# Attention, soft mixture of experts and MLP on one core: four buffers for whole chunks of P, two for the light ones, four for x, and no quarter of expert weights loaded ahead

## The chip, the core and the metric

The kernel runs on one core of a Trainium2 chip. A core has five engines that each take their own instructions in order: PE (TensorE, matmuls; the profile lists its weight loads apart as PEld), ACT (ScalarE), DVE (VectorE), POOL (GpSimd) and SP (SyncE, which here only issues DMA transfers). Semaphores tie them together. The metric is the time of one execution on the device in microseconds (us), as the median of several runs. Before the change it is 596.64 us, the median of three runs from 596.44 to 599.81 us.

## The reference

Attention over 4 batches of 12 heads with 448 positions and 64 channels, with scores squeezed by a tanh; then a soft mixture of 8 experts with 4 slots each; then an MLP with a leaky activation. All in fp32.

```python
scores = cap * np.tanh(scale * (q @ k.T) / cap)
attn = np.exp(scores - scores.max(-1)); attn /= attn.sum(-1) + 1e-09
x = (attn @ v)                                    # to 1792 x 768
logits = x @ phi                                  # phi: 768 x 32 slots
d = softmax(logits, over tokens); c = softmax(logits, over slots)
slot_input = d.T @ x                              # 4 rows for each of 8 experts
slot_out[e] = np.maximum(slot_input[e] @ w1[e], 0.0) @ w2[e]
x = c @ slot_out
h = x @ w_in
out = (np.maximum(h, 0.0) + alpha * np.minimum(h, 0.0)) @ w_out
```

## The kernel before, in words

**Attention** takes the heads two at a time, 24 pairs in all. The 448 keys of a pair are cut into four chunks: three whole ones (0, 1, 2) of 128 keys, with both heads side by side in 896 columns, and a light one (3) that holds the last 64 keys of both heads in 448 columns. A step g does, for pair i and the next chunk in `CHUNKS = (0, 3, 1, 2)`: `qk` (three matmul passes into the PSUM tile `s`, of which there are two, then on ACT a tanh, L395, and an exp, L396, into a tile `p` of P), then what `later` put down for this step, then loads, and then, two steps behind (`LAG = 2`), `pv` of an older chunk: P times V into the one PSUM bank `o`. Step 1 of a pair also transposes the next pair's k and q (`tr`).

`pv` of chunk 1 makes POOL add up P for the row sums: `acc = p0 + p1` (L412, one add for each head) and then the light chunk's rows (L415); `pv` of chunk 2 adds the third whole chunk (L419). ACT then copies `o` to SBUF as `xu` (L421), and only then may PE write `o` for the next pair. The tiles of P come from two pools that are used in turn: `pt`, three buffers for whole chunks, and `ptt`, one buffer for light ones. A tanh may write a buffer when PE and POOL have read what was in it.

`xu` has five buffers. It is kept until `norm` (DVE, L502) multiplies it by the inverse row sums, which come for three pairs together: `norm` of pairs 0, 1, 2 falls on steps 20, 24 and 28.

In the background DVE and ACT convert `w_in` from float64, which passes through `cvbuf` (`conv_w_in`, L192 to L203), and SP loads q, k and v two pairs ahead.

**Weights.** The experts' weights (50 MB) go through eleven slots of 12 KB per partition in a pool `arena`. `LOADS` lists the pairs at whose last step a slot's load is issued, if a slot is free: ten are, and the eleventh (the one that holds `cvbuf`) comes free at pair 22. So the pairs that load are 2, 4, ... 20 and 22. Beyond the slots there is a quarter, `early` (one tile of 3 KB per partition), into which `load_early` loads the first quarter of the next piece (w2 of expert 2) at pair 21. All loads are on SP's queue. When attention ends, its memory becomes seven more slots (`xslots`), each filled as soon as what lay there is read for the last time (L119); from then on a slot that an expert has finished with is refilled at once.

**Tail.** `experts` runs the eight experts, `gather` turns the result, and `mlp` does the rest on PE, DVE and ACT. `mlp` uses a scratch tile `more`, for which it takes the memory of `early`.

Of the kernel before, what the change touches and what calls it, by code (L numbers as in the profile page):

```python
# [8 lines left out]
F32 = mybir.dt.float32  # L9
# [15 lines left out]
def tile_attention_soft_moe_mlp(ctx, tc, q, k, v, cap, phi, w1, w2, w_in, w_out, alpha, out):  # L25
# [5 lines left out]
    NPAIR = B * NP  # L31
    NT, DM = out.shape
# [9 lines left out]
    SLOT = 3072  # L42
    NA = 11
    NX = 7
    QE = 1
    JK = 3
    KEYS = 128 * JK
    TAIL = S - KEYS
# [3 lines left out]
    LAG = 2  # L52

    CHUNKS = (0, 3, 1, 2)
    LOADS = (2, 4, 6, 8, 10, 12, 14, 16, 18, 20, 21, 22)

    EH = 5
    TBS = (4, 2, 2, 2, 2, 2)
# [4 lines left out]
    arena = ctx.enter_context(tc.tile_pool(name="arena", bufs=1))  # L63
# [10 lines left out]
    slotT = const.tile([128, KD, NSLOT], F32, name="slotT")  # L74
    w_in32 = dram_p.tile([DFF // 512, DM, 512], F32, name="w_in32")
    xslots = []
    early = [arena.tile([128, SLOT // 4], F32, tag=f"early{c}", name="w") for c in range(QE)]

    def slot(i, shape, dtype=F32, name="w"):
        return arena.tile(shape, dtype, tag=f"slot{i}", name=name)  # L80
# [2 lines left out]
    loads, rest = [], []  # L83
# [11 lines left out]
    where = {}  # L95
# [18 lines left out]
    def load_part(kind, e, i, c, t, after=None):  # L114
        if kind == "w2":
            src = w2_rows(e, i)[:, c // 2, c % 2]
        else:
            src = w1_rows(e, i)[:, c]
        ins = nc.sync.dma_start(out=t, in_=src)  # L119
        if after is not None:  # L120
            tc.add_manual_dep(ins.ins, after.ins.name, NOSYNC, reason="prefetch pace")
        return t

    def load_early(after):

        key = loads[NA]
        where[key] = [load_part(*key, c, t, after) for c, t in enumerate(early)]

    def load_next(after=None):
        slot_no = may_load()  # L130
# [110 lines left out]
    def attention():  # L241
        with ExitStack() as pools:
            def pool(name, bufs=1, **kw):
                return pools.enter_context(tc.tile_pool(name=name, bufs=bufs, **kw))
# [4 lines left out]
            v_0 = pool("vn0")  # L249
            acc_0 = pool("acc0")  # L250
            stk_1 = pool("stk1")
            pt_p = pool("pt", 3)
            ptt_p = pool("ptt")
            v_1 = pool("vn1")
            acc_1 = pool("acc1")
            ac0_p = pool("aconst0")
            xn_p = pool("xn", 7)
            xu_p = pool("xu", 5)
            xnat_p = pool("xnat", 2)
            sm_p = pool("sm")  # L260
            ac_p = pool("aconst")
# [22 lines left out]
            nat, stk, sc_t, pt, acc, ov, xu, xn = {}, {}, {}, {}, {}, {}, {}, {}  # L284
# [399 lines left out]
            def cv_at(n):  # L684
                return cv_steps[n]
# [39 lines left out]
            last = None  # L725
            for g in range(NPAIR * J + LAG):
                now[0] = g
                i, c = divmod(g, J)
                if g == 14:
                    nc.sync.dma_start(out=alpha_sb, in_=alpha.rearrange("(k p) -> p k", p=128))  # L730
                if g == 17:
                    nc.vector.tensor_scalar(out=nalpha_sb, in0=alpha_sb, scalar1=-1.0, scalar2=None, op0=ALU.mult)
                if i < NPAIR:
                    qk(i, CHUNKS[c])
                    if c == 1 and i + 1 < NPAIR:
                        trans_k(i + 1)
                        trans_q(i + 1)
                run_bg()
                if i < NPAIR:
                    if c == 0:  # L740
                        last = load(i + 2, "kq") or last
                    if c == 2:
                        if i == NPAIR - LAG - 1:
                            load_early(last)
                    for n in range(ncv):
                        if cv_at(n) == g - 2:
                            store_w_in(n)
                        if cv_at(n) == g:
                            conv_w_in(n)
                    if c == 3 and i in LOADS and may_load() is not None:  # L750
                        load_next(last)
                if g >= LAG:
                    n, e = divmod(g - LAG, J)
                    pv(n, CHUNKS[e])
                    if e == J - 1:
                        load(n + 2, "v")
# [22 lines left out]
    def tail():  # L779
# [3 lines left out]
        def unit(n, dtype, name):  # L783
            return r2[0].tile([128, DM], dtype, tag=f"u{n}", name=name)
# [50 lines left out]
        def experts(which, small, ps_w, yacc, cstk=None):  # L835
            for e in which:
                if e == E - 1:
                    to_single(0)
                    split_wo(0)
                hT = small[:, 0:256].rearrange("p (u j s) -> p u j s", u=2, j=4)  # L840
                nc.gpsimd.memset(hT, 0.0)
                h1 = ps_w.tile([128, 512], F32, tag="w", name="h1")[:, :256]
                for kk in range(KD):
                    wv = where["w1", e, kk // 3]
                    for j in range(4):
                        nc.tensor.matmul(
                            h1[32 * j:32 * j + 32, :],
                            slotT[:, kk, :],
                            wv[kk % 3][:, 256 * j:256 * j + 256],
                            start=(kk == 0),  # L850
                            stop=(kk == KD - 1),
                            tile_position=(0, 32 * j),
                        )
                done_with("w1", e, 0)
                done_with("w1", e, 1)
                rl = small[:, 256:512]
                nc.scalar.activation(
                    out=rl.rearrange("q (u p) -> q p u", u=2), in_=h1.rearrange("q (p u) -> q p u", u=2), func=AF.Relu
                )
                tp = ps_w.tile([128, 512], F32, tag="w", name="tp")[:, :256]  # L860
                for u in range(2):
                    nc.tensor.transpose(tp[:, 128 * u:128 * u + 128], rl[:, 128 * u:128 * u + 128], ident)
                nc.vector.tensor_copy(
                    out=hT[:, :, :, SPE * e:SPE * e + SPE],
                    in_=tp.rearrange("p (u j s) -> p u j s", u=2, j=4)[:, :, :, SPE * e:SPE * e + SPE],
                )
                for kk in range(KE):
                    wv = where["w2", e, kk // 4]
                    for g in range(G3):
                        pe[0] = nc.tensor.matmul(  # L870
                            yacc[32 * g:32 * g + 32, :256],
                            hT[:, kk % 2, kk // 2, :],
                            wv[kk % 4][:, 256 * g:256 * g + 256],
                            start=(e == 0 and kk == 0),
                            stop=(e == E - 1 and kk == KE - 1),
                            tile_position=(0, 32 * g),
                        )
                done_with("w2", e, 0)
                done_with("w2", e, 1)
                if EH <= e < EH + B // 2:  # L880
                    for b in (2 * (e - EH), 2 * (e - EH) + 1):
                        build_c(b, ps_w, cstk)
# [433 lines left out]
        with (  # L1316
            tc.tile_pool(name="ps_w", bufs=2, space=PSUM, reuse_waits="tile") as ps_w,
            tc.tile_pool(name="ps_c", bufs=6, space=PSUM, reuse_waits="tile") as ps_c,
        ):
            yacc = ps_c.tile([128, 512], F32, tag="c", name="y")  # L1320
            with (
                tc.tile_pool(name="ex2", bufs=1, reuse_waits="tile", side="right") as ex2_p,
                tc.tile_pool(name="xtra", bufs=1, reuse_waits="tile") as xt_p,
            ):
                small = ex2_p.tile([128, 512], F32, name="small")
                xslots.append(xt_p)
                free.extend(range(NA, NA + NX))
                load_free()
                experts(range(EH), small, ps_w, yacc)
            with (  # L1330
                tc.tile_pool(name="r2", bufs=1, reuse_waits="tile") as r2_p,
                tc.tile_pool(name="ex", bufs=1, reuse_waits="tile") as ex_p,
                tc.tile_pool(name="gg", bufs=1, reuse_waits="tile") as g_p,
            ):
                r2.append(r2_p)
                so = ex_p.tile([128, KD, 2, NSLOT], F32, name="so")
                cstk = ex_p.tile([128, NT], F32R, name="cstk")
                a_stk = ex_p.tile([128, DFF], F32R, name="a_stk")
                gr = g_p.tile([128, 4096], F32R, name="gr")
                gs = g_p.tile([128, 2688], F32, name="gs")  # L1340
                ob = g_p.tile([128, 2, DM], F32, name="ob")
                experts(range(EH, E), unit(6, F32, "small"), ps_w, yacc, cstk)
                gather(ps_w, yacc, so)
                more = arena.tile([128, SLOT // 4], F32, tag="early0", name="more")
                mlp(ps_w, ps_c, so, cstk, a_stk, gr, gs, ob, more)

    attention()
    tail()


# [28 lines left out]
```

## Time and profile before

| | |
|---|---|
| median of three runs | 596.64 us |
| the profiled execution: its own time | 595.48 us |
| its span, first to last instruction | 593.6 us |
| PE busy | 554.3 us, 93% of the span |
| DVE / ACT / POOL busy | 433.9 / 377.4 / 169.4 us |
| attention, about 12 to 273 us | PE, ACT, DVE and POOL all work |
| experts, to 336 us | the 16 DMA engines are full |
| MLP, 339 us to the end | PE is full |

Busy time is a share over stages with different limits, so what a change is worth is read from its own stage. "Idle before" and the waits say what an engine waited for last; matmuls are pipelined and their ends are modelled. "PEclk" is the TensorE clock that was granted, as a share of 2.4 GHz.

### The profile page before, as it was taken

The numbers are of one execution on the slowest core, as the hardware profiler recorded it, in microseconds if no ns is written. First come the engines' busy times: TensorE is split into PE (matmuls) and PEld (weight loads), VectorE is DVE, ScalarE is ACT, GpSimd is POOL, SyncE is SP. The second block draws the span as 40 slices with busy tenths as digits, with TensorE's granted clock in tenths as the row PEclk, the third lists the DMA queues.
The fourth block names the chain that finished last, engine by engine and source line by source line (L and its number), as shares of the span: only waits on it lengthen the run. The fifth ranks groups of instructions, "written<-read, shape, count | busy, mean of one in ns | idle before, by whom it ended". The sixth has DMA issues, their size and how long they took to land.

```text
span 593.6 us, 10809 instructions
## 1 busy us (share of the span) xinstructions
PE 554.3 (93%) x4008; PEld 383.4 (65%) x4008; DVE 433.9 (73%) x834; ACT 377.4 (64%) x617; POOL 169.4 (29%) x158
## 2 busy tenths in 40 slices
PE   5979998999999999988888989999999999999996
PEld 4434444455545445445445568878888999999996
DVE  3688976788577958562011499999999979797974
ACT  3988888888888978831011157764777855565651
POOL 0786877766765656510000000000000000000000
PEclk9998999999999999999999999999999999999999
DMA  6577887888787784599999999500030101010101
GB/s 174 115 249 214 268 254 236 209 252 250 231 204 222 241 237 109 193 376 386 421 420 418 396 399 412 204 0 1 20 88 1 55 0 55 2 53 1 54 1 54
DMA packets 83461, 110.93 MB, mean 187 GB/s; under 512 B 55376, under 2 KB 63312, under 8 KB 81872
## 3 DMA queue, kind: packets, MB, share of 16 engines
q1 hardware_dynamic: 81168, 109.28, 55.8%
q10 hardware_dynamic: 2240, 0.95, 0.6%
q8 instruction: 32, 0.52, 0.4%
q14 instruction: 21, 0.17, 0.1%
HBM read 98.41 MB, written 11.80 MB: 186 GB/s over the span
## 4 chain that ended last, share of the span: by engine, by line
PE 66%; DMA 10%; ACT 10%; POOL 6%; DVE 3%; issue 2%; SPq 1%; ACTq 0%
DMA w<-in_moe_w_dram 9%; PE o L293 8%; PE s L293 7%; PE P L1204 6%; PE P L1206 6%; PE P L1205 6%; PE oc L979 6%; PE oc L985 6%; PE oc L986 6%; ACT p L396 3%; POOL acc L412 3%; POOL acc L415 3%; ACT p L395 2%; PE aps L907 2%; PE nx L293 2%
## 5 line engine op out<-in xcount | busy, mean ns | idle before, releaser
L293 PE MATMUL o<-p,v 128*64 128x448 f32 (+1 forms) x384 | 94.0, 568 | 11.1 <-ACT xu L421 11.0
L395 ACT ACTIVATE p<-s 128x896 f32<-128x896 f32 x96 | 79.1, 824 | 29.0 <-PE s L293 17.7
L396 ACT ACTIVATE p<-p,cap 128x896 f32<-128x896 f32 x96 | 91.1, 950 | 2.4
L412 POOL TENSOR_TENSOR acc<-p 128x448 f32<-128x448 f32 x48 | 58.0, 1230 | 68.3 <-ACT p L396 68.3
L985 PE MATMUL oc<-wsp,gr 128*128 128x512 f32 (+1 forms) x192 | 64.9, 339 | 0.0
L986 PE MATMUL oc<-wsp,gr 128*128 128x512 f32 (+1 forms) x192 | 64.2, 337 | 0.0
L979 PE MATMUL oc<-wsp,gr 128*128 128x512 f32 (+1 forms) x192 | 62.0, 340 | 0.0
L293 PEld LDWEIGHTS s<-qh,kh 64*128 64x128 f32 (+1 forms) x168 | 18.2, 187 | 67.3 <-issue 24.7
L1195 ACT ACTIVATE gr<-gs 128x384 fp32r<-128x384 f32 (+1 forms) x64 | 36.6, 575 | 32.8 <-DVE gs L1179 26.8
L415 POOL TENSOR_TENSOR acc<-acc,p 64x448 f32<-64x448 f32 x46 | 54.5, 1184 | 1.7
L419 POOL TENSOR_TENSOR acc<-acc,p 128x448 f32<-128x448 f32 x46 | 54.0, 1195 | 1.8
L1196 DVE TENSOR_TENSOR gr<-gs,gr 128x384 fp32r<-128x384 f32 x64 | 39.1, 619 | 17.4 <-ACT gr L1195 17.4
L293 PE MATMUL s<-qh,kh 64*128 64x448 f32 (+1 forms) x168 | 46.0, 476 | 0.0
L1204 PE MATMUL P<-wsp,gr 128*128 128x384 f32 x128 | 42.9, 335 | 0.0
L1205 PE MATMUL P<-wsp,gr 128*128 128x384 f32 x128 | 42.8, 334 | 0.0
L1206 PE MATMUL P<-wsp,gr 128*128 128x384 f32 x128 | 42.8, 334 | 0.0
L293 PEld LDWEIGHTS o<-p,v 128*64 128x64 f32 (+1 forms) x384 | 19.0, 134 | 36.3 <-ACT xu L421 17.8
L979 PEld LDWEIGHTS oc<-wsp,gr 128*128 128x128 f32 x192 | 36.2, 190 | 5.4 <-ACT wsp L814 0.8
L985 PEld LDWEIGHTS oc<-wsp,gr 128*128 128x128 f32 x192 | 36.4, 189 | 5.1 <-DVE wx L203 0.4
L986 PEld LDWEIGHTS oc<-wsp,gr 128*128 128x128 f32 x192 | 36.3, 189 | 4.4 <-issue 0.4
L293 PE MATMUL s<-ql,kh 64*128 64x448 f32 (+1 forms) x168 | 35.5, 366 | 1.0 <-DVE ql L375 1.0
L293 PE MATMUL s<-qh,kl 64*128 64x448 f32 (+1 forms) x168 | 35.6, 366 | 0.0
(234 smaller groups left out, 1228.3 us busy)
## 6 DMA issues: line engine op xcount, KB each, us to landing
w<-in_moe_w_dram SPq DMA_DIRECT2D x26, 768.0 KB, 12.5
w<-in_moe_w_dram SPq DMA_DIRECT2D x12, 1536.0 KB, 11.8
cvbuf<-in_moe_w_in_dram SPq DMA_DIRECT2D x24, 512.0 KB, 5.3
w<-in_moe_w_out_dram SPq DMA_DIRECT2D x16, 768.0 KB, 10.4
w_in<-cvbuf SPq DMA_DIRECT2D x24, 256.0 KB, 2.7
w<-in_moe_w_dram SPq DMA_DIRECT2D x12, 512.0 KB, 6.2
q<-in_q_dram SPq DMA_DIRECT2D x44, 112.0 KB, 4.1
k<-in_k_dram SPq DMA_DIRECT2D x48, 96.0 KB, 5.5
```

Source lines behind the costliest of these rows:

```text
L293: ins = nc.tensor.matmul(*a, **kw)
L395: nc.scalar.activation(out=pe, in_=ps[:, :n, :S], func=AF.Tanh)
L396: nc.scalar.activation(out=pe, in_=pe, func=AF.Exp, scale=cap_sb)
L412: nc.gpsimd.tensor_add(out=a[:, u, :], in0=pt[i, 0][:, u, :], in1=pe[:, u, :])
L415: nc.gpsimd.tensor_add(out=a[r, u, :], in0=a[r, u, :], in1=pt[i, JK][r, 0, :])
L419: nc.gpsimd.tensor_add(out=a[:, u, :], in0=a[:, u, :], in1=pe[:, u, :])
L979: ins = nc.tensor.matmul(o, gh[:, ts], wo_h[f][:, cols], start=(f == 0 and not second), stop=False)
L985: nc.tensor.matmul(o, gh[:, ts], wo_l[f][:, cols], start=False, stop=False)
L986: nc.tensor.matmul(o, gl[:, ts], wo_h[f][:, cols], start=False, stop=(f == KF - 1 and not more))
L1204: nc.tensor.matmul(o, hi[:, i], bh, start=(p == 0), stop=False)
L1205: nc.tensor.matmul(o, hi[:, i], bl, start=False, stop=False)
L1206: nc.tensor.matmul(o, lo[:, i], bh, start=False, stop=(p == 7))
```

## The change

Buffers: `pt` 3 to 4 (3,584 bytes per partition each), `ptt` 1 to 2 (1,792), `xu` 5 to 4 (2,048), and the tile `early` (3,072) goes. The sum is 256 bytes more. `more` gets a tile of its own after attention. `load_early` is gone, so that quarter is loaded with the first of the extra slots. The loads for the ten slots go out at pairs 4, 6, ... 18, 19, 20 in place of 2, 4, ... 20; the eleventh stays at 22.

```diff
-    QE = 1
-    LOADS = (2, 4, 6, 8, 10, 12, 14, 16, 18, 20, 21, 22)
+    LOADS = (4, 6, 8, 10, 12, 14, 16, 18, 19, 20, 21, 22)
-    early = [arena.tile([128, SLOT // 4], F32, tag=f"early{c}", name="w") for c in range(QE)]
-    def load_early(after):
-
-        key = loads[NA]
-        where[key] = [load_part(*key, c, t, after) for c, t in enumerate(early)]
-            pt_p = pool("pt", 3)
-            ptt_p = pool("ptt")
+            pt_p = pool("pt", 4)
+            ptt_p = pool("ptt", 2)
-            xu_p = pool("xu", 5)
+            xu_p = pool("xu", 4)
-                    if c == 2:
-                        if i == NPAIR - LAG - 1:
-                            load_early(last)
+                more = g_p.tile([128, DM], F32, name="more")
-                more = arena.tile([128, SLOT // 4], F32, tag="early0", name="more")
```

On ACT, one pair in the early part of attention, before the change. `p<-s` is a tanh (896 columns: whole, 448: light), `p<-p,cap` the exp after it; what stands in brackets are the engines and queues whose semaphores it waits for.

```order
95 L395 ACTIVATE p<-s 128x896 [waits PE_49,Pool_49]
96 L396 ACTIVATE p<-p,cap 128x896 [waits Activation_49]
97 L395 ACTIVATE p<-s 128x896 [waits PE_49,Pool_49]
98 L396 ACTIVATE p<-p,cap 128x896 [waits Activation_49]
99 L395 ACTIVATE p<-s 128x448 [waits PE_49,Pool_49]
100 L396 ACTIVATE p<-p,cap 128x448 [waits Activation_49]
101 L360 ACTIVATE kh<-tr 128x512 [waits DVE_49,PE_49]
102 L192 ACTIVATE cvbuf<-cvbuf 128x512 [waits DMAHW4_49,DMAHW3_49,DVE_49]
103 L421 ACTIVATE xu<-o 128x448 [waits DVE_49,PE_49]
104 L395 ACTIVATE p<-s 128x896 [waits PE_49]
```

The same place with the change.

```order
95 L388 ACTIVATE p<-s 128x896 [waits PE_49]
96 L389 ACTIVATE p<-p,cap 128x896 [waits Activation_49]
97 L388 ACTIVATE p<-s 128x896 [waits PE_49,Pool_49]
98 L389 ACTIVATE p<-p,cap 128x896 [waits Activation_49]
99 L388 ACTIVATE p<-s 128x448 [waits PE_49]
100 L353 ACTIVATE kh<-tr 128x512 [waits PE_49]
101 L389 ACTIVATE p<-p,cap 128x448 [waits Activation_49]
102 L185 ACTIVATE cvbuf<-cvbuf 128x512 [waits DMAHW3_49,DMAHW2_49]
103 L414 ACTIVATE xu<-o 128x448 [waits DVE_49,PE_49]
104 L388 ACTIVATE p<-s 128x896 [waits PE_49,Pool_49]
```

The light tanh (row 99) and that of chunk 2 (row 95) no longer wait for POOL. That of chunk 0 (row 97) waited for the add L412 of the pair just before; it now waits for L419 of the pair before that one. That of chunk 1 (row 104) now waits for L412 of the pair just before, where it waited for no add. The copy to `xu` (row 103) waits for a `norm` that comes one tile later than before.

On SP, the transfers behind attention's last ones, before the change (`w` are the experts' weights; 768, 1024, 1536 and 3072 are columns of 128 partitions).

```order
183 L695 DMA w_in_72<-cvbuf 128x512
184 L171 DMA w<-in_moe_w_dram 128x1536 x2
185 L119 DMA w<-in_moe_w_dram 128x768 x3
186 L119 DMA w<-in_moe_w_dram 128x1024 x6
187 L119 DMA w<-in_moe_w_dram 128x768 x8
```

And with the change.

```order
182 L688 DMA w_in_72<-cvbuf 128x512
183 L164 DMA w<-in_moe_w_dram 128x1536 x2
184 L117 DMA w<-in_moe_w_dram 128x768 x4
185 L117 DMA w<-in_moe_w_dram 128x1024 x6
186 L117 DMA w<-in_moe_w_dram 128x768 x8
```

The fourth transfer of 768 columns is the quarter that `load_early` brought in at pair 21.

## Rows read from the trace of the kernel before

**Rows 1.** Windows: us; busy PE, PEld, DVE, ACT, POOL (instructions); PEclk, DMA share, GB/s.

```profile
22.60:60.60 38.00, 33.40 (x207) 15.11 (x206) 32.73 (x43) 33.49 (x46) 29.12 (x24) 0.96 0.74 216
60.60:109.20 48.60, 43.68 (x281) 20.76 (x280) 38.21 (x54) 41.71 (x56) 37.16 (x31) 1.00 0.86 250
109.20:248.10 138.90, 133.49 (x972) 66.81 (x972) 106.78 (x185) 116.42 (x163) 92.23 (x80) 1.00 0.73 208
```

**Rows 2.** Timeline of ACT: light tanh of pairs 1, 10 and 23 (start, us).

```profile
22.63 0.54 ACT L395 ACTIVATE p<-s 128x448 f32<-128x448 f32 x1
...
109.20 0.54 ACT L395 ACTIVATE p<-s 128x448 f32<-128x448 f32 x1 [0.33 <-POOL acc L415]
...
248.10 0.54 ACT L395 ACTIVATE p<-s 128x448 f32<-128x448 f32 x1 [1.55 <-PE s L293]
```

**Rows 3.** Waits of ACT, 22.6 to 109.2 us: total us, times, longest.

```profile
ACT p L395 <- POOL acc L415: 4.3, 8, 1.1
ACT p L395 <- POOL acc L412: 4.2, 6, 1.2
ACT cvbuf L192 <- DMA cvbuf<-in_moe_w_in_dram: 1.6, 1, 1.6
```

**Rows 4.** Waits of PE, 22.6 to 109.2 us.

```profile
PE o L293 <- ACT xu L421: 8.7, 9, 2.3
```

**Rows 5.** Timeline of POOL, then of ACT and PE, at pairs 4 and 5.

```profile
56.32 2.25 POOL L412 TENSOR_TENSOR acc<-p 128x448 f32<-128x448 f32 x2 [3.04 <-ACT p L396]
58.52 2.62 POOL L415 TENSOR_TENSOR acc<-acc,p 64x448 f32<-64x448 f32 x2
61.22 3.02 POOL L419 TENSOR_TENSOR acc<-acc,p 128x448 f32<-128x448 f32 x2
65.73 1.16 POOL L412 TENSOR_TENSOR acc<-p 128x448 f32<-128x448 f32 x1 [1.49 <-ACT p L396]
...
61.17 0.55 ACT L395 ACTIVATE p<-s 128x448 f32<-128x448 f32 x1 [0.57 <-POOL acc L415]
...
64.95 0.58 PE L293 MATMUL rs<-acc,hot 128*32 128x224 f32 x8
```

**Rows 6.** Waits of PE and ACT, 109.2 to 248.1 us.

```profile
PE o L293 <- ACT xu L421: 2.3, 6, 0.6
...
ACT p L395 <- PE s L293: 12.1, 16, 1.7
```

**Rows 7.** Windows around the lowest granted clock.

```profile
44.50:50.00 5.50, 5.50 (x30) 1.88 (x28) 4.13 (x6) 3.67 (x5) 3.73 (x4) 0.69 0.89 291
```

**Rows 8.** Timeline of ACT and DVE: a copy to xu, and DVE around it.

```profile
62.65 0.54 ACT L421 ACTIVATE xu<-o 128x448 f32<-128x448 f32 x1
...
54.32 0.69 DVE L203 SCALAR_TENSOR_TENSOR cvbuf<-cvbuf 128x512 uint32<-128x512 uint32 x1
61.72 1.52 DVE L203 SCALAR_TENSOR_TENSOR cvbuf<-cvbuf 128x512 uint32<-128x512 uint32 x1
63.16 0.61 DVE L502 TENSOR_TENSOR xn<-xu,rb 128x448 f32<-128x448 f32 x1
```

**Rows 9.** Timelines of SP and PE: a load of k behind weights, and its transposes.

```profile
77.16 0.93 SPq L171 DMA_DIRECT2D w<-in_moe_w_dram  x2
78.13 0.58 SPq L337 DMA_DIRECT2D k<-in_k_dram  x1
...
89.30 0.49 PE L293 MATMUL tr<-ident,k 128*128 128x128 f32 x3
```

**Rows 10.** DMA issues, 77 to 90 us: count, KB each, median us to landing.

```profile
k<-in_k_dram SPq DMA_DIRECT2D x4, 96.0 KB, 7.4
```

**Rows 11.** Windows of the stage that loads the experts; the chain's longest piece there.

```profile
258.00:262.00 4.00, 3.90 (x17) 1.55 (x16) 3.06 (x5) 0.54 (x1) 0.00 (x0) 1.00 0.83 286
262.00:336.40 74.40, 64.45 (x881) 37.12 (x882) 16.20 (x46) 11.39 (x26) 2.49 (x8) 1.00 1.02 409
...
317.49 18.81 DMA w<-in_moe_w_dram
```

## The prediction

> **What bounds the kernel now.** I read the windows by stage first, then who waited for whom, then the timeline where the waits are. The windows [rows 1] cut attention at light tanhs [rows 2], one per pair: pairs 1 to 9 take 109.20 - 22.63 = 86.6 us (9.6 each), pairs 10 to 22 take 138.9 us (10.7 each). In the late part PE is busy 133.5 of 138.9 us: PE bounds it. In the early part nothing is full: PE is busy 33.4 + 43.7 = 77.1 us of 86.6, ACT 33.5 + 41.7 = 75.2, DVE 70.9, POOL 66.3. There the waits close a circle. ACT waits 4.3 + 4.2 = 8.5 us for POOL's adds and 1.6 us for one transfer [rows 3]; PE waits 8.7 us for ACT's copy to xu [rows 4]. The timeline shows a turn [rows 5]: POOL starts L412 at 56.32, L415 ends at 61.14, and at 61.17 the light tanh starts, 0.57 us after it could. What ACT then has to do before the next exp of chunk 1 brings POOL to its next L412 at 65.73: a turn of 9.4 us, about the pair's 9.6. So early attention runs at the pace of a loop through POOL and ACT, which exists because the light piece of P has one buffer and chunk 0 comes back to its own after three.
>
> After attention the experts' loads fill the DMA engines (share 1.02, 409 GB/s), and the chain goes through transfers until 336 us [rows 11]; the MLP behind it is PE's alone and isn't touched. Both start when attention lets them: what attention gains is passed on to the end.
>
> **The change part by part.** The sum is made against the profiled execution's own 595.48 us; the runs' median, 596.64, lies 1.16 above, and I shift by that at the end.
>
> *Buffers of P (pairs 1 to 9).* The order on ACT shows the light tanh without a wait for POOL, and those of chunks 0 and 1 waiting for adds about a pair old. POOL needs 2.25 + 2.62 + 3.02 = 7.9 us in the pair shown [rows 5], 66.3 / 9 = 7.4 on average [rows 1], so at 9 us a pair it keeps up. What PE gets back is the part of its 8.7 us for xu that came from ACT running late. Bounds: nothing, if ACT is late by its own work (75.2 us against PE's 77.1, nearly the same); or all but what the late pairs show, where PE waits 2.3 us in 13 pairs, 0.18 each [rows 6], so 8.7 - 9 x 0.18 = 7.1. I take 0.33 a pair as the rest, nearer to the late pairs (same program, the POOL waits all but gone) but above them, because ACT has slack there (12.1 us of waiting for PE's scores [rows 6]) that it lacks here: 8.7 - 3.0 = **-5.7**.
>
> *Clock.* From 44.5 to 50 us the granted clock is 0.69 [rows 7], a mix of the two levels 1.2 and 2.4 GHz, just behind PE's longest wait for xu, 2.3 us [rows 4]. Over 22.6 to 60.6 us the clock is 0.96 [rows 1], so 0.04 x 38 = 1.5 us of PE's work is lost. With shorter waits it may not fall. Between 0 and 1.5: **-0.8**.
>
> *Four buffers of xu.* The fifth copy now takes the first's buffer and must wait until `norm` of pair 0 has read it. In the trace that copy starts at 62.65 and this `norm` ends at 63.77 [rows 8]: ACT will wait 1.1 us, with kh, exp and the next tanhs queued behind, and PE's `o` too. At later pairs the `norm` is due one step ahead of the copy. Bounds 0 (ACT has slack after all) and 3 us (as much at two more pairs): **+1.1**.
>
> *The ten loads, one or two pairs later.* The first, at pair 2, goes away there: the 1.6 us that ACT waited for cvbuf [rows 3] fall in pair 3 behind it (within the -5.7, as ACT's lateness). Elsewhere there are as many loads as before until pair 18, then three in a row. But the pairs get shorter while bytes don't: DMA share is 0.86 from 60.6 to 109.2 us [rows 1], 8.3 us of each 9.6. Behind a weights load, k issued at 78.13 [rows 9] lands after some 7.4 us in the median [rows 10], the q and kt behind it later, and PE transposes it at 89.30 [rows 9], a margin of 3.8 us at most; at 9.0 us a pair the five steps between shrink by 0.7 us. Bounds 0 and 3: **+0.8**. The three loads in a row fall where the share is far lower (0.73 on average [rows 1]), and I cost them at nothing; without that cover each would hold k and q for its own 1.57 MB / 409 GB/s = 3.8 us.
>
> *Late pairs.* PE waits 2.3 us for xu there [rows 6]; a third of it goes: **-0.7**, between 0 and -2.3.
>
> *The quarter not loaded ahead.* 128 x 768 x 4 B = 0.393 MB move behind attention, where the engines are full: 0.393 / 409 GB/s = 0.96 us. Against it stand 4 us at share 0.83 [rows 11], where SP waits for attention's memory: 0.17 x 4 = 0.7 us of room, partly filled by a longer queue. Between 0.3 and 1.0: **+0.7**.
>
> The Trainium skill (DMA: Bandwidth & Descriptors, Specifications) gives a core about 358 GB/s of HBM; by that the quarter would cost 1.1 us, and the sum would be 0.1 later. The rows, at 409 GB/s over 74 us, go above that figure, and the measurement decides.
>
> `more` in a tile of its own costs nothing: it is first written deep in the MLP. Order on PE stays the same.
>
> Sum: -5.7 - 0.8 + 1.1 + 0.8 - 0.7 + 0.7 = -4.6 us, so 590.9 for this execution, and on the runs' median **592.0 us**.
>
> **The rivals.**
>
> *PE's own work becomes the pace (more gain).* All but 0.18 us a pair of the xu waits goes, the clock doesn't fall, and the costs stay small: -7.1 - 1.5 - 1.0 + 1.5 = -8.1, so 588.5. For it: ACT's 75.2 us would just fit into PE's 77.1. Against it: even the late pairs, where ACT has slack, don't run without this wait.
>
> *Given back inside attention.* The transfers become the pace of pairs 5 to 9 (share 0.86), or POOL still does: the row sums of pair 4 start on PE at 64.95, only 0.7 us after POOL's L419 (61.22 + 3.02 = 64.24) has ended [rows 5]; with ACT freed, PE would wait for POOL in ACT's place. That is the way in which the change would not do what it says. Then only pairs 1 to 4 gain, 4/9 of 5.7 = 2.5, and the rest is costs and small gains that cancel: 594.5. Against it: POOL's 7.4 us and the transfers' 8.3 us are both below 9.
>
> *Slower: xu's fourth buffer is missed in every group.* ACT would wait for DVE at most copies from pair 4 on. DVE is 70.9 of 86.6 us busy, and where POOL runs it gets slower: the same conversion takes 0.69 us, and 1.52 us beside L419 [rows 8, 5]. With POOL no longer pacing ACT, `norm` could fall back. It decides the sign when the waits reach 4.6 + 1.1 = 5.7 us, over 19 copies 0.3 us each; at 0.6 us each it is 592.0 + 19 x 0.6 - 1.1 = 602. Against it: in the program each `norm` stands a step ahead of the copy that needs it, and DVE does no more than before.
>
> The Trainium skill states such a rule (SBUF — State Buffer, on the shared port pair): DVE with two SBUF inputs and GpSimd lock each other out for a whole instruction. The trace agrees with 0.69 against 1.52 us. By that rule alone a faster pace puts the same blocked time into a shorter pair, which is this rival.
>
> **How the numbers follow.** A difference of about 1% (6 us) is what a measurement of this kernel can tell from none; the bounds are 590.7 and 602.6 us. My forecast, 589.7 to 594.3, has a chance of 0.45; the sum of its terms is good to some 2 us. More gain (587 to 589.7): 0.22. Given back (594.3 to 597.5): 0.22. Slower than that: 0.11, of which 0.04 beyond 602.6. Faster by over 1% is all of the second and about a quarter of the first: 0.22 + 0.11 = 0.33; slower by over 1% 0.04; the rest, 0.63, within 1%. The range from 588.0 to 597.5 leaves out about 0.11 above and 0.08 below.
>
> **What would show it.** In the profile after: no wait of ACT's tanh for POOL, light tanhs 8.9 to 9.1 us apart in pairs 1 to 9, PE's wait for xu near 3 us there, one wait of an early xu copy for a `norm` of about 1 us, no low clock near 45 us. The late pairs keep 10.6 to 10.7 us. The experts' last transfer lands about 5 us earlier than 336. I'm wrong if the light tanhs keep 9.6 us with PE waiting for transfers or for POOL's sums, or if the gain in attention isn't seen at the end of the loads.

## The result, and the profile after

The changed kernel takes 593.31 us (median of 18 runs, 588.94 to 595.35); the kernel before, on the same chip, 597.54 us (18 runs, 594.87 to 601.39). The ratio is 0.9909, with a 95% interval from 0.9887 to 0.9932: 0.7 to 1.1% faster. The forecast of 592.0 us, against 596.64, was a gain of 0.8%.

The table cuts both profiled executions at the same events: the light tanhs (one per pair), the first matmul `h` of the experts and the end of the last `y`.

| stretch | before, us | after, us | difference |
|---|---|---|---|
| start to light tanh of pair 1 | 22.63 | 22.11 | -0.5 |
| pairs 1 to 9 | 86.57 | 81.68 | -4.9 |
| pairs 10 to 22 | 138.90 | 138.33 | -0.6 |
| pair 23 and attention's end, to the first `h` | 24.93 | 25.39 | +0.5 |
| experts, first `h` to last `y` | 64.38 | 65.97 | +1.6 |
| the rest, to the end of the span | 256.2 | 256.2 | 0.0 |
| span | 593.6 | 589.7 | -3.9 |

In attention the changed kernel's lines are numbered 7 lower: L388 and L389 are the tanh and the exp (before L395, L396), L405, L408 and L412 are POOL's three adds (before L412, L415, L419), L414 is the copy to `xu` and L495 the `norm`.

The light tanhs of pairs 1, 10 and 23 after the change, from ACT's timeline (start, duration, what was computed):

```profile
22.11 0.52 ACT L388 ACTIVATE p<-s 128x448 f32<-128x448 f32 x1
...
103.79 0.54 ACT L388 ACTIVATE p<-s 128x448 f32<-128x448 f32 x1
...
242.12 0.54 ACT L388 ACTIVATE p<-s 128x448 f32<-128x448 f32 x1 [1.48 <-PE s L286]
```

The windows between them, with the columns of [rows 1]:

```profile
22.10:60.60 38.50, 35.14 (x213) 16.06 (x210) 37.95 (x43) 33.71 (x48) 35.39 (x27) 0.96 0.75 214
60.60:103.80 43.20, 42.62 (x273) 19.93 (x271) 36.59 (x52) 41.23 (x56) 33.82 (x28) 1.00 0.83 235
103.80:242.10 138.30, 133.86 (x975) 67.05 (x975) 106.93 (x187) 116.54 (x163) 93.56 (x81) 1.00 0.76 223
```

Against [rows 1], PE's idle time in pairs 1 to 9 fell from 86.6 - 77.1 = 9.5 us to 81.7 - 77.8 = 3.9 us. From 60.6 us on PE is busy for 42.62 of 43.2 us: it is the pace there now. In the first window the engine that is full is DVE, with 37.95 of 38.5 us.

Who waited, first ACT and then PE, in the early pairs (20 to 103 us) of the changed kernel:

```profile
ACT p L388 <- PE s L286: 4.5, 6, 1.8
ACT cvbuf L185 <- DMA cvbuf<-in_moe_w_in_dram: 1.0, 1, 1.0
```

```profile
PE o L286 <- ACT xu L414: 1.9, 5, 0.7
PE s L286 <- DVE qh L367: 1.2, 1, 1.2
PE s L286 <- DVE ql L368: 0.6, 1, 0.6
```

ACT's 8.5 us of waits for POOL [rows 3] are gone, and ACT now waits for PE. PE's wait for xu fell from 8.7 us [rows 4] to 1.9. In its place stand 1.8 us of waits for DVE, in one pair. The timelines of PE, DVE and POOL show that place:

```profile
54.65 0.47 PE L286 MATMUL s<-qh,kh 64*128 64x448 f32 x2 [1.19 <-DVE qh L367]
55.74 0.47 PE L286 MATMUL s<-ql,kh 64*128 64x448 f32 x2 [0.62 <-DVE ql L368]
```

```profile
51.66 0.69 DVE L193 SCALAR_TENSOR_TENSOR cvbuf<-cvbuf 128x512 uint32<-128x512 uint32 x1
52.39 1.51 DVE L196 SCALAR_TENSOR_TENSOR cvbuf<-cvbuf 128x512 uint32<-128x512 uint32 x1
53.83 0.67 DVE L367 TENSOR_SCALAR qh<-tr,tscale 128x448 fp32r<-128x448 f32 x1
...
55.02 0.67 DVE L368 SCALAR_TENSOR_TENSOR ql<-tr,tscale,qh 128x448 fp32r<-128x448 f32 x1
...
57.69 1.51 DVE L193 SCALAR_TENSOR_TENSOR cvbuf<-cvbuf 128x512 uint32<-128x512 uint32 x1
...
52.18 2.72 POOL L405 TENSOR_TENSOR acc<-p 128x448 f32<-128x448 f32 x2 [0.83 <-ACT p L389]
...
57.45 2.76 POOL L412 TENSOR_TENSOR acc<-acc,p 128x448 f32<-128x448 f32 x2
```

DVE converts `w_in` before it gets to the next pair's q, and is late with both halves of it. The same conversion step, L193, takes 0.69 us at 51.66, where POOL mostly waits for ACT, and 1.51 us at 57.69, beside POOL's L412; [rows 8] have the same for another step. The Trainium skill (SBUF — State Buffer, two separate sides) names a cause: DVE with two SBUF inputs and GpSimd exclude each other from a shared port pair. The two durations agree with it; no run without POOL's adds tests it.

### The profile page after: what moved, and what is told of

Its sections match the earlier page's. It is cut to its first block, busy times and chain, and to the rows that moved or that the text cites. A ratio compares the mean times of both kernels' runs of the same rounds, so it can differ in the third digit from the quotient of the medians.

```text
span 589.7 us, 10780 instructions
## 1 busy us (share of the span) xinstructions
PE 557.1 (94%) x4008; PEld 385.1 (65%) x4008; DVE 437.7 (74%) x834; ACT 377.0 (64%) x617; POOL 173.1 (29%) x158
## 4 chain that ended last, share of the span: by engine, by line
PE 78%; DVE 9%; ACT 6%; DMA 3%; issue 2%; SPq 1%; ACTq 0%; DVEq 0%
PE o L286 9%; PE s L286 8%; PE P L1196 7%; PE P L1194 6%; PE P L1195 6%; PE oc L969 6%; PE oc L975 6%; PE oc L976 6%; PE y L860 5%; PE h L836 4%; PE aps L897 2%; PE nx L286 2%; ACT p L389 2%; PE rs L286 2%; ACT p L388 2%
## 5 line engine op out<-in xcount | busy, mean ns | idle before, releaser
L388 ACT ACTIVATE p<-s 128x896 f32<-128x896 f32 x96 | 78.6, 819 | 23.7 <-PE s L286 20.7
L389 ACT ACTIVATE p<-p,cap 128x896 f32<-128x896 f32 x96 | 91.0, 948 | 2.2
L405 POOL TENSOR_TENSOR acc<-p 128x448 f32<-128x448 f32 x48 | 60.1, 1273 | 59.0 <-ACT p L389 59.0
L976 PE MATMUL oc<-wsp,gr 128*128 128x512 f32 (+1 forms) x192 | 64.1, 337 | 0.0
L408 POOL TENSOR_TENSOR acc<-acc,p 64x448 f32<-64x448 f32 x46 | 55.3, 1203 | 1.7
L412 POOL TENSOR_TENSOR acc<-acc,p 128x448 f32<-128x448 f32 x46 | 54.7, 1209 | 1.8
L286 PEld LDWEIGHTS o<-p,v 128*64 128x64 f32 (+1 forms) x384 | 19.0, 134 | 27.9 <-issue 11.6
L847 ACT ACTIVATE small<-h 128x256 f32<-128x256 f32 x8 | 4.9, 610 | 48.6 <-PE h L836 48.6
```

The costliest lines, as they stand in the source:

```text
L286: ins = nc.tensor.matmul(*a, **kw)
L388: nc.scalar.activation(out=pe, in_=ps[:, :n, :S], func=AF.Tanh)
L389: nc.scalar.activation(out=pe, in_=pe, func=AF.Exp, scale=cap_sb)
L405: nc.gpsimd.tensor_add(out=a[:, u, :], in0=pt[i, 0][:, u, :], in1=pe[:, u, :])
L408: nc.gpsimd.tensor_add(out=a[r, u, :], in0=a[r, u, :], in1=pt[i, JK][r, 0, :])
L412: nc.gpsimd.tensor_add(out=a[:, u, :], in0=a[:, u, :], in1=pe[:, u, :])
```

## The experiments

Ratios are to the kernel before, timed beside it on the same chip. "Pairs 1 to 9" is the distance of the light tanhs of pairs 1 and 10 in the profiled execution (before 86.6, after 81.7 us).

### Which part of the change brings the gain

Three runs put buffers of P back. The rest of the change stays in each.

```diff
 a1_pt3_ptt1:  pt 4 -> 3, ptt 2 -> 1
 a2_ptt1:      ptt 2 -> 1
 a3_pt3:       pt 4 -> 3
```

> The change with its two rings of P put back (pt 3, ptt 1); four xu, no quarter ahead and the later loads stay. If the gain comes from the rings (theory A), the loop through POOL is back: ACT's waits for POOL near 8 us in pairs 1 to 9, light tanhs 9.4 to 9.6 us apart, ratio to before 0.998 to 1.003. If it comes from the load that pair 2 no longer issues (theory B), the ratio stays at 0.990 to 0.994.

Measured: 596.98 us, ratio 0.9988 [0.9965, 1.0012], pairs 1 to 9 in 84.6 us. Without the new buffers of P nothing is left that can be told from no change. The light tanhs are 9.4 us apart, as expected; the waits for POOL, 6.1 us, are shorter than the 8 expected. ACT's and PE's waits, 22.4 to 107 us, show the loop back in place, and with it the wait for `norm` that the fourth xu buffer brings:

```profile
ACT p L388 <- POOL acc L405: 3.1, 6, 0.9
ACT p L388 <- POOL acc L408: 3.0, 7, 0.8
ACT xu L414 <- DVE xn L495: 1.1, 1, 1.1
```

```profile
PE o L286 <- ACT xu L414: 9.1, 9, 2.4
```

> The change with one buffer for light pieces (ptt 1), four for whole chunks. Theory A as I put it: the loop passes through L415 and the light tanh, so with one light buffer it stands almost as before: waits for L415 4 us or more in pairs 1 to 9, ratio 0.996 to 1.000. If the whole chunks' third buffer was what held ACT (theory A2), the gain stays: ratio 0.990 to 0.993.

Measured: 595.91 us, 0.9979 [0.9958, 1.0000], pairs 1 to 9 in 84.4 us. The fourth buffer for whole chunks brings nothing that can be told from zero as long as the light piece has one: ACT's wait for POOL only moves from L405 to L408.

```profile
ACT p L388 <- POOL acc L408: 6.1, 8, 1.8
```

> The change with three buffers for whole chunks (pt 3), two for light pieces. The tanh of chunk 0 waits for L412 of the pair before, some 0.5 us a pair where the light one waited more. Theory A: part of the gain is left, ratio 0.993 to 0.997, ACT's waits for L412 4 to 5 us in pairs 1 to 9 and none for L415. Theory A2: the gain is gone, ratio 0.998 to 1.001.

Measured: 593.48 us, 0.9930 [0.9905, 0.9955], pairs 1 to 9 in 82.3 us. The second light buffer alone, with the rest of the change, has most of the gain; the fourth whole buffer adds at most some 0.2% (0.9930 against 0.9909, intervals that overlap). ACT waits 2.4 us for L405 and never for L408; 4 to 5 us were expected for the first.

The fourth run puts the old times of the loads back and keeps all the new buffers.

```diff
-    LOADS = (4, 6, 8, 10, 12, 14, 16, 18, 19, 20, 21, 22)
+    LOADS = (2, 4, 6, 8, 10, 12, 14, 16, 18, 20, 21, 22)
```

> The change with the old list of loads (pairs 2, 4, ... 20, 22). Theory A: the same as the change within 0.2% (ratio 0.990 to 0.993), with ACT's wait for cvbuf longer by some 0.6 to 2 us at pair 3. Theory B: the gain is gone, ratio 0.997 to 1.000.

Measured: 597.59 us, 0.9990 [0.9964, 1.0016], pairs 1 to 9 in 83.8 us: the whole gain is gone. My theory, which gave 0.990 to 0.993, fell. The waits of ACT (20.9 to 104.7 us) and of PE (104.7 to 146.3 us) show where it went:

```profile
ACT cvbuf L185 <- DMA cvbuf<-in_moe_w_in_dram: 4.6, 3, 2.5
ACT xu L414 <- DVE xn L495: 1.7, 1, 1.7
```

```profile
PE tr L286 <- DMA k<-in_k_dram: 1.2, 1, 1.2
...
PE tr L286 <- DMA kt<-in_k_dram: 0.3, 1, 0.3
```

ACT has no wait for POOL here, but 4.6 us for the transfers of `cvbuf` in place of 1.6 [rows 3], and PE waits 6.7 us for xu again. PE waits 1.5 us for k and kt at 106 us, and the granted clock from 104.7 to 120 us is 0.89:

```profile
104.70:120.00 15.30, 13.72 (x77) 6.15 (x77) 8.81 (x15) 10.14 (x14) 10.13 (x9) 0.89 0.89 241
```

From the light tanh of pair 10 to that of pair 11, 13.8 us pass in place of 10.6 after the change. So with POOL out of the way, the old load times hold ACT and PE at a few places: pair 3, where the longest wait for cvbuf falls, takes 12.7 us in place of 9.9, and pair 10 loses 3.2 us, in part to the clock. Pairs 6 to 9 keep 8.6 to 9.4 us, so transfers aren't the pace throughout. The clock over a whole run is also lower, 0.985 to 0.991 with a median of 0.986, against a median of 0.991 before.

### The other parts, each alone on the kernel before

Three runs change one thing each in the kernel before.

```diff
 b3_lateloads:  LOADS as in the change
 b1_noquarter:  no load_early, `more` in a tile of its own
 b2_xu4:        xu 5 -> 4
```

> The kernel before with only the ten loads moved to the later pairs. My prediction's step on this part (costs nothing, takes the wait for cvbuf away): ratio 0.997 to 1.000, pairs 1 to 9 at 85.5 to 86.6, no wait of ACT for cvbuf, the waits for POOL still 8 to 9 us. If the later loads help by themselves (the transfers were the pace already before the change): ratio 0.991 to 0.995 and pairs 1 to 9 below 84.5.

Measured: 595.11 us, 0.9975 [0.9953, 0.9997], pairs 1 to 9 in 83.9 us. The ratio is at the expected place. The pairs are shorter than expected: ACT's wait for cvbuf is gone, and its waits for POOL (22.8 to 106.7 us) fell as well, to 6.6 us.

```profile
ACT p L395 <- POOL acc L415: 3.8, 7, 1.1
ACT p L395 <- POOL acc L412: 2.8, 6, 0.9
```

The later loads alone gain 0.25%. The two runs that have one of the two steps each, a1 (loads) and a4 (buffers of P), also have the fourth xu buffer taken away, as in b2 below. So they are read against b2's 1.0039 (b2 still loads the quarter ahead; b1 puts that at 0.1%, within its interval): the loads gain 0.5%, the buffers of P 0.5%, both together 1.3%. Most of that simply adds up, and the 0.3% beyond the sum is within the intervals. What hints at more is PE's idle time in pairs 1 to 9, the first number of a row less the second, in one profile each of b2, a1 and a4:

```profile
22.55:110.01 87.46, 77.88 (x483) 36.01 (x480) 69.77 (x96) 75.50 (x101) 65.91 (x54) 0.96 0.81 232
23.04:107.63 84.59, 75.54 (x485) 35.55 (x484) 68.63 (x96) 75.34 (x102) 64.87 (x54) 1.00 0.79 224
20.87:104.71 83.84, 76.47 (x477) 34.99 (x477) 71.97 (x93) 74.99 (x101) 67.47 (x55) 0.98 0.81 236
```

It is 9.6 us in b2, 9.1 with the loads, 7.4 with the buffers and 3.9 with both. That would fit two limits that lie close behind each other; the times don't show it.

> The kernel before without the quarter loaded ahead (and more in a tile of its own), old rings, five xu, old loads. My price: 0.3 to 1.0 us at the experts' last transfer, ratio 1.000 to 1.002; nothing at all if the experts' end is not set by transfers when the clock falls ahead of them.

Measured: 597.56 us, 1.0010 [0.9989, 1.0030]. Loading the quarter behind attention costs nothing that can be told from zero; the interval, -0.7 to +1.8 us, holds my price too.

> The kernel before with four buffers of xu in place of five, and nothing else. My price: ACT waits 1.1 us for a norm at pair 4, ratio 1.000 to 1.002. If the fourth buffer were missed in every group, waits of 0.3 us or more at most copies and a ratio over 1.005.

Measured: 599.87 us, 1.0039 [1.0019, 1.0059], pairs 1 to 9 in 87.5 us: slower, by more than expected. ACT's wait is the one I had worked out, at one copy and for 1.1 us:

```profile
ACT xu L421 <- DVE xn L502: 1.1, 1, 1.1
```

By the ratio the cost is 2.3 us. The profile shows where the rest can come from. PE waits 1.7 us for this copy, and behind that the granted clock is 0.72 for 6 us, where it is 1.00 in the profile before:

```profile
64.17 0.97 PE L293 MATMUL o<-p,v 128*64 128x448 f32 x4 [1.68 <-ACT xu L421]
...
64.00:70.00 6.00, 5.83 (x30) 2.12 (x30) 4.55 (x8) 4.59 (x7) 3.33 (x3) 0.72 0.97 251
```

That is 0.28 x 6 = 1.7 us of PE's work. It fits that the clock over a whole run is lower, 0.987 in the mean of b2's 12 runs and 0.990 in that of the kernel before beside them; no run of its own shows it, and in a1, where ACT waits the same 1.1 us and PE 1.2, the clock stays at 1.00 from 64 to 70 us. The same wait of ACT stands in a1, a2, a3 and a4. In the changed kernel itself it doesn't appear, probably because there PE, and with it the copy, is later at that place (the waits for qh and ql above).

### Where the gain is given back

The experts took 1.6 us longer after the change. PE's timeline at attention's end, after the change:

```profile
261.67 0.40 PE L286 MATMUL nd<-ident,ls 32*112 32x32 f32 x4 [1.82 <-ACT ls L574]
...
267.51 4.68 PE L836 MATMUL h<-w,slotT 128*32 128x256 f32 x48
```

and the windows there:

```profile
260.00:264.00 4.00, 1.99 (x54) 1.72 (x54) 2.21 (x9) 1.44 (x4) 0.00 (x0) 1.00 1.03 407
264.00:272.00 8.00, 7.65 (x70) 4.89 (x62) 2.83 (x11) 0.31 (x1) 0.31 (x1) 0.57 1.03 406
```

PE waits 1.82 us for ACT, and behind that wait the granted clock is 0.57 for 8 us: most of it at 1.2 of the two levels 1.2 and 2.4 GHz. The first 48 matmuls `h` take 4.7 us there, and 2.8 in the profiled execution before. That execution waits the same 1.8 us at the same place, with a clock of 1.00 behind it:

```profile
267.65 0.40 PE L293 MATMUL nd<-ident,ls 32*112 32x32 f32 x4 [1.82 <-ACT ls L581]
...
267.60:275.60 8.00, 7.26 (x116) 5.61 (x116) 4.24 (x16) 1.02 (x3) 0.31 (x1) 1.00 1.02 380
```

So I added matmuls that nothing reads, ahead of the wait, to the kernel after (c1) and to the one before (b4).

```diff
+    WARM = 12
...
+                keep = ps_o.tile([128, 512], F32, tag="o", name="warm")
+                for _ in range(WARM):
+                    matmul(keep[:, :128], ident, ident, start=True, stop=True)
                 softmax_d(B - 1, ls, ps)
```

> The change plus twelve 128x128 matmuls on PE into the bank of o, where PE waits for ACT at attention's end; the profiles of the change and of four variants show the granted clock at 0.83 over 260 to 280 us, that of before 1.00. If PE's wait of 1.8 us there lets the clock fall (theory C), it stays at 1.00 in that stretch, the first expert takes 7.8 in place of 9.9 us, and the ratio to before is 0.984 to 0.988. If the fall has another reason (theory D), the clock stays at 0.83 and the ratio at 0.989 to 0.993.

Measured: 590.94 us (590.02 to 591.43), 0.9880 [0.9856, 0.9905]. The wait is filled, the clock stays up, and the experts take 64.1 us in place of 66.0:

```profile
260.00:264.00 4.00, 3.63 (x42) 3.40 (x44) 2.60 (x9) 1.44 (x4) 0.00 (x0) 1.00 1.03 408
264.00:272.00 8.00, 6.79 (x110) 5.02 (x105) 2.98 (x11) 0.92 (x2) 0.31 (x1) 1.00 1.03 407
```

> The kernel before with only the twelve 128x128 matmuls behind the last logits (extra work, nothing reads it). Theory: the low granted clock at the end of attention belongs to the kernel before as well in most of its executions, and the change didn't bring it: clock 1.00 from 260 to 280 us, ratio 0.994 to 0.998, as much as the change gained by the same matmuls (0.991 to 0.988). But before, the transfers end the experts' stage, so part of the gain may stay hidden there. Rival: the low clock came with the change: ratio 0.999 to 1.002.

Measured: 596.47 us (594.31 to 597.43), 0.9987 [0.9973, 1.0002]. The ratio is between what the two theories gave and settles nothing. In the profile the low clock wasn't taken away but came later:

```profile
264.00:272.00 8.00, 7.41 (x97) 6.37 (x94) 4.63 (x15) 2.35 (x6) 0.00 (x0) 1.00 1.00 369
272.00:280.00 8.00, 7.01 (x67) 4.00 (x70) 1.15 (x6) 0.61 (x1) 0.31 (x1) 0.79 1.00 371
```

That the change didn't bring the low clock is shown by another run: b1, with the old buffers and the old loads, has it too.

```profile
272.00:280.00 8.00, 7.26 (x59) 3.73 (x61) 1.57 (x7) 0.92 (x2) 0.00 (x0) 0.61 1.02 404
```

In the profiles of all experiments without the extra matmuls the granted clock over 260 to 280 us is 0.74 to 0.83. The profiled execution before, at 1.00, was the exception among these profiles, and I had forecast from it.

### The conversions on DVE

After the change the light tanhs of pairs 3, 4, 5 and 6 lie 9.9, 11.9 and 8.6 us apart, those behind them 8.8. DVE is full there, and the first eight conversions follow each other at a distance of three steps, where a pair has four; behind step 29 every fourth step has one. (The expectation below splits the same 30 us of pairs 3 to 5 as 9.9, 10.2 and 10.1.) Two runs move conversions.

```diff
-            cv_steps = [4, 7, 10, 13, 16, 19, 22, 25, 29]
 c2_cv:       4, 8, 12, ... 64, then 67, 70, ... 85, and 89
 e2_cvsteps:  2, 4, 7, 10, 13, 17, 21, 25, 29, then every 4th step
```

> The change with the conversions of w_in one per pair up to step 64 and every third step from 67 to 85, in place of every third step up to 25 and one per pair after. In the change pairs 3 to 5 take 9.9, 10.2 and 10.1 us (waits for the transfer to cvbuf, for DVE's qh and ql, a low clock), pairs 6 to 9 8.8. If the crowded conversions are why (theory E), pairs 3 to 5 go to 8.5 to 8.9 us each and the ratio to before is 0.982 to 0.987. If the first pairs are slow for the loads or the clock alone, the ratio stays at 0.989 to 0.993.

Measured: 602.34 us, 1.0080 [1.0050, 1.0111]. Pairs 3 to 5 take 8.4, 9.6 and 8.6 us, near what was expected, and pairs 1 to 9 take 79.3. But pairs 10 to 22 take 149.87, 11.5 us more than with the change, and 4.3 of these are PE busy for longer, at a granted clock of 0.98. PE's longest waits from 101.4 to 251.3 us:

```profile
PE nx L286 <- DVE kl L354: 2.9, 2, 2.6
PE rb L286 <- DVE xnat L510: 2.8, 2, 2.5
...
PE lr L286 <- DVE xn L495: 1.4, 1, 1.4
```

The light tanhs of pairs 11 and 12, 17 and 18, and 19 and 20 lie 13.5, 15.3 and 16.8 us apart, after the change 11.6, 11.6 and 12.2. PE waits there for DVE's work on x at the end of a batch of six pairs (xnat, xn), and on the next pair's k (kl). That the conversions now meet this work, or from step 67 on lie too close, is argued from the steps and was tried only so far that e2, which keeps the late steps, has none of it.

> The change with only the conversions moved (steps 2, 4, 7, 10, 13, 17, 21, 25, 29, then every fourth). Theory: DVE's crowding held pairs 3 to 5: pairs 1 to 9 at 78.5 to 80 against 81.7, no wait of PE for qh or ql, late pairs 138 to 139; with the low clock at the attention's end still there, ratio 0.984 to 0.988. Rival: the pace comes from elsewhere, ratio 0.989 to 0.993, as with the change alone.

Measured: 592.22 us, 0.9914 [0.9887, 0.9942], pairs 1 to 9 in 81.4 us: no different from the change, the rival's numbers. The late pairs keep 137.9 us. DVE from 20 to 60 us tells why, in e2 and then in c2:

```profile
20.00:60.00 40.00, 36.23 (x227) 16.93 (x226) 38.96 (x42) 37.84 (x52) 37.54 (x29) 1.00 0.73 203
```

```profile
20.00:60.00 40.00, 38.67 (x243) 17.97 (x243) 35.07 (x41) 37.52 (x52) 34.13 (x29) 1.00 0.71 194
```

Moving one conversion ahead leaves DVE full over all of these 40 us (38.96), and PE's wait only goes to another tile. Where the steps are spread (c2), DVE has 35.07 us of work there and PE gets 38.67. So DVE as a whole, not one crowded pair, holds the first five pairs.

> The change, with two additions: twelve 128x128 matmuls into the unused bank o behind the last logits (extra work, nothing reads it), and the conversions of w_in at steps 2, 4, 7, 10, 13, 17, 21, 25, 29 and every fourth step after that, so that no pair of the early part gets two. Theory: the early pairs 3 to 5 (9.9 to 10.2 us with the change) were held by DVE where two conversions fell into one pair, and the late pairs suffered in the run with conversions at every fourth step from 4 because the conversions then meet the batch ends. Then pairs 1 to 9 take 78.5 to 80, pairs 10 to 22 stay at 138 to 139, the granted clock is 1.00 from 260 to 280 us, and the ratio to the kernel before is 0.980 to 0.985. Rival: what held pairs 3 to 5 returns from another engine (PE's wait for xu): pairs 1 to 9 at 81 to 82, ratio 0.986 to 0.989, as with the twelve matmuls alone.

Measured, with both additions: 589.16 us (588.93 to 590.29), 0.9870 [0.9853, 0.9887], pairs 1 to 9 in 81.4 us. This is the fastest kernel of the study, but it can't be told from c1. Its experts took 65.8 us, with a clock of 0.79 from 264 to 272 us, so the extra matmuls don't always keep the clock up. What they do to the times is seen over the runs: 590.02 to 591.43 (c1) and 588.93 to 590.29 (e1), five runs each, where the change alone runs from 588.94 to 595.35. The nearest comparison is e1 with e2, timed beside each other, which differ by the matmuls alone: 589.16 against 592.22 us, with a clock over the whole run of 0.996 to 1.000 against 0.987 to 0.999. The fastest single run, 587.95 us, is one of e2's, at 0.999.

## Why the prediction was right, point by point

**Buffers of P: -5.7.** Right in mechanism and nearly in size. ACT's waits for POOL are gone; PE's wait for xu fell by 6.8 us, its idle time by 5.6. A rest of 3.0 us was forecast for xu, and 1.9 + 1.8 = 3.7 stand there for xu and DVE together. The prediction put all of this on the rings. a1 to a3 show that, of the rings, the second light buffer brings most, with little from the fourth whole one. But the rings bring it only together with the later loads: with the old ones (a4) PE still waits 6.7 us for xu, and its idle time falls to 7.4 us and not to 3.9.

**The loads: at nothing.** This step failed. I weighed what the new times of the loads cost and not what the old ones would have cost once POOL no longer paced attention. With them the change is worth nothing that can be told (a4: 0.9990), so with the new rings in place the move of the loads carries about 0.8%, 0.9990 - 0.9909; without them it carries 0.25% (b3) to 0.5% (a1 against b2). In the prediction's own terms, the 1.6 us for cvbuf weren't a part of ACT's lateness that goes with the rings: they grow to 4.6 when the old loads stay (a4). That the sum held is in part luck: what I gave to the rings alone needs both steps, and the change happened to have both.

**Transfers: +0.8.** PE waits once in the late pairs for a transfer of q, 0.4 us, so it cost less. The rival in which the transfers take the gain back inside attention has a ground, though: with the old load times they do so at a few places (a4). (Its number was off: with the rest cancelling, 596.64 - 2.5 is 594.1, not 594.5.)

**Four buffers of xu: +1.1.** Right in place and, for the wait, in size (1.1 to 1.7 us in a1 to a4 and b2); after the change it doesn't appear, probably hidden behind the 1.8 us for DVE. What the buffer costs was mis-sized: 2.3 us by b2's ratio, the part beyond the wait perhaps by the clock.

**Clock: -0.8.** This didn't come. The low stretch near 45 us [rows 7] is gone, but another lies at 54 to 60 us, just behind PE's waits for DVE. And the stretch near 45 us wasn't the rings': b1 and b3, with the old rings and a longest wait for xu of 2.3 us too, have a clock of 1.00 there, and b1 takes 85.3 us for pairs 1 to 9, 1.3 less than the profiled execution before.

```profile
44.50:50.00 5.50, 5.11 (x33) 2.74 (x31) 5.40 (x7) 4.50 (x8) 5.35 (x4) 1.00 0.72 184
54.00:60.00 6.00, 4.73 (x16) 2.43 (x17) 5.90 (x8) 2.63 (x3) 5.85 (x5) 0.72 0.97 348
```

After the change the clock over 22.1 to 60.6 us is 0.96, as before [rows 1]. The rings, the clock and xu together were forecast as -5.4 us, -4.6 with the transfers; pairs 1 to 9 gained 4.9.

**Late pairs: -0.7.** They gained 0.6; PE's wait for xu fell from 2.3 us [rows 6] to 0.7.

```profile
PE o L286 <- ACT xu L414: 0.7, 3, 0.3
...
PE tr L286 <- DMA q<-in_q_dram: 0.4, 1, 0.4
```

**The quarter: +0.7.** Nothing that b1 can tell from zero, with an interval that holds 0.7 too. The step rested on the chain that goes through transfers until 336 us [rows 11]. The chain named what came last, by little: PE has no row of waiting for `w` in the experts' stage, before or after. The waits are the same few (after, 255 to 340 us):

```profile
PE tp L852 <- ACT small L847: 6.3, 8, 0.8
PE nd L286 <- ACT ls L574: 1.8, 1, 1.8
```

So the step that what attention gains is passed on to the end was right, but by way of PE. Of the 5.5 us by which the experts start earlier, 3.9 arrive; 1.6 go to the low clock, which I had not put in.

**The rival on the other side** (xu missed at most copies) didn't come: one copy waits, in the runs that show it. But its ground was sound, since the changed kernel's first five pairs are held by DVE beside POOL.

## What to carry to other kernels

When a ring of buffers is deepened, look for the limit that lies next behind it, and try to move that one too: here the change without the new rings (a1) and the change without the later loads (a4) both end at 0.999, the whole at 0.991. When two parts are tested by taking one out, ask what else stays in: both of these runs also carry the 0.4% that the fourth xu buffer costs. A chain of waits names what came last, not by how much; before a stage is called bound by transfers, look for the engine's own waits for them. And read the clock of several executions before forecasting from one.

## What the runs showed that I had not expected

The time of a run goes with its mean granted clock. The 18 runs of the changed kernel lie between 588.94 us at 0.999 and 595.35 us at 0.984, which is more than the change gains. The same 1.8 us wait of PE at attention's end was followed by a clock of 1.00 in one profile and of 0.57 over 8 us in another. What decides between them stays open, and so does whether c1's gain over the change, 0.9880 against 0.9909 with intervals that overlap, is more than chance; e1 against e2 speaks for it. Also left open is whether five buffers of xu beside the new rings would be faster still; that wasn't tried.
